# TensorE's order pinned by unit in an attention and MLP kernel, with VectorE's steps of masks and outputs queued behind each unit's maxima

## The chip, the cores and the metric

The kernel runs on one core of one Trainium2 chip. The metric is the device time of one execution in microseconds (us), as the median over several executions. Five engines work side by side, each through its own instructions in order: TensorE (PE, with its weight loads listed apart as PEld), VectorE (DVE), ScalarE (ACT), GpSimd (POOL) and SyncE (SP), which issues the DMAs. TensorE writes its results to PSUM, which is cut into banks, and the others read them from there.

## The reference

Attention in which a query sees only the keys of its own cluster, then a token-mixing and a channel-mixing MLP, then a second mixing block with a cosine and a sine of a projection. Cut to what matters:

```python
# attention: B, H, S, D = 2, 8, 768, 64; 16 clusters
q_assign = np.argmax(np.einsum('bhsd,hcd->bhsc', q_n, c_n), axis=-1)
k_assign = np.argmax(np.einsum('bhsd,hcd->bhsc', k_n, c_n), axis=-1)
mask = q_assign[:, :, :, None] == k_assign[:, :, None, :]
scores = scale * np.matmul(q, k.transpose(0, 1, 3, 2))
scores = np.where(mask, scores, -1000000000.0)
attn = np.exp(scores - np.max(scores, axis=-1, keepdims=True))
attn = attn / (np.sum(attn, axis=-1, keepdims=True) + 1e-09)
x = np.matmul(attn, v)                      # then heads side by side: (2, 768, 512)
# first block: w_tok1 768x256, w_tok2 256x768, w_ch1 512x1536, w_ch2 1536x512
h = np.maximum(x.transpose(0, 2, 1) @ w_tok1, 0.0) @ w_tok2
u = x + h.transpose(0, 2, 1)
x = u + np.maximum(u @ w_ch1, 0.0) @ w_ch2
# second block
theta = x @ w_theta
y = np.einsum('ts,bsd->btd', w_tok_r, x * np.cos(theta)) + np.einsum('ts,bsd->btd', w_tok_i, x * np.sin(theta))
u = x + y
out = u + np.maximum(u @ w_ch, 0.0)
```

## The kernel before

The attention is cut into 48 units: a head and a block of 256 of its 768 queries, three units to a head, six to a pair of heads. A unit has three kinds of work on TensorE. **Scores** (`scores`) are two halves of 128 queries, each in one of two PSUM banks `s`, each made of four products: L397 and L398, where L398 adds the cluster mask and the low parts of the split operands. VectorE takes the maximum of a half (`nm`, L400), ScalarE the exponential (`e`, L402), which reads the bank for the last time. **Transposes** (`turn`) are twelve (L417), in three groups that each fill one of three banks `t`; the first two groups are copied out by ScalarE (`p`, L420), the third by VectorE (L422). **Values** (`values`) are twelve products (L438) into the single bank `o`; ScalarE copies one half of it (`tmp`, L445) and VectorE adds the other (`xt`, L447), the last reader of that bank.

The units are staged by `SKEW = 2`: step n of the loop issues the scores of unit n, the transposes of unit n-1 and the values of unit n-2. Between them stand other things. A generator `masks` makes the masks of the next pair of heads in six pieces, two to a step (`PACE`): eight `sim` products into a bank `t` (L246), four VectorE steps, a product `pp` (L270), and `oh` and `m` (L271, L286), which DMAs from SP place in the operands of the next pair's scores. `natural` takes the finished outputs of a pair of heads back to rows: VectorE makes the reciprocal sums `ri` (L455, L456), TensorE six transposes `x` (L460) into two banks `t`, VectorE scales them into `xn` (L462). In the last steps the weights of the first MLP are loaded (`load_w`, L109 to L116, of which L109 and L110 are on ScalarE, L112 and L113 on VectorE, L116 on GpSimd) and, near the end, its first products are made by `tok_up` (`g` in PSUM, then `gh` on ScalarE, L147, and `gl` on VectorE, L148) and `tok_down` (`h`). The inputs of these are split into high and low parts `xh` (L84) and `xl` (L86). Every MLP product is three matmuls (`mm3`, L126 to L128).

A scheduler that runs when the kernel is built decides the order of the instructions on each engine. `tc.issue_after(ins)` puts whatever is issued under it behind the instruction `ins` on the same engine: an edge of order, not a semaphore. `marks` keeps such instructions by name: `marks["scores"]`, `marks["max"]`, `marks["turn"]` are the latest score product, maximum and transpose.

## Time and profile before

| | us |
|---|---|
| median of the runs shown | 665.26 (663.36, 665.26, 665.73) |
| profiled execution | 664.99 |
| its span | 663.3 |
| TensorE busy | 646.8 (98%) |
| weight loads busy | 517.7 (78%) |
| VectorE busy | 401.2 (60%) |
| ScalarE busy | 344.9 (52%) |
| GpSimd busy | 257.6 (39%) |

The span goes from the first to the last instruction of the profiled execution, and its own time is 1.7 us longer. Busy times of matmuls overlap a little, since one starts before the one ahead of it has ended, so distances are best read from start to start. In the rows below PEclk and clock stand for the granted clock of TensorE as a share of full speed, and "[0.62 <-ACT e L402]" behind a row means that the engine was idle for 0.62 us ahead of it and that ScalarE's `e` of line 402 ended this.

### The profile page before, as it was taken

To read this page: it belongs to the slowest core of one execution; us is meant where nothing else is said; L and a number is where in the kernel's file an instruction comes from. 1 tells how busy PE (TensorE), PEld (TensorE's weight loads), DVE (VectorE), ACT (ScalarE), POOL (GpSimd) and SP (SyncE) were. 2 spreads that over 40 slices of the span, in tenths; PEclk is the share of its full clock that TensorE was granted. 3 is DMA by queue.
4 is the path that set the end of the run, shared out by engine and by line. 5 is a ranking of instruction groups with operands and counts; after the bars stand their busy time and mean duration, and the time that the engine had idled before them with its cause. 6 is when DMAs were issued, how large, how long until landed. Compare 5 with 4: busy or idle time off the path is not lost.

```text
span 663.3 us, 9795 instructions
## 1 busy us (share of the span) xinstructions
PE 646.8 (98%) x3591; PEld 517.7 (78%) x3591; DVE 401.2 (60%) x649; ACT 344.9 (52%) x653; POOL 257.6 (39%) x231
## 2 busy tenths in 40 slices
PE   7999999999999989999999999999999999999998
PEld 4777777777777758878888888888887878888886
DVE  5877778687787776466665442546677694531212
ACT  5676776777767863256444320428487673320000
POOL 6230312364031131138887520603467796541000
PEclk9999999999999998999999999999999999999999
DMA  8554755444555121023433310310021424300001
GB/s 294 160 138 105 169 123 144 120 117 114 113 123 124 37 96 47 18 67 124 154 133 127 126 53 14 95 33 0 1 85 42 128 88 127 114 20 33 16 33 47
DMA packets 24207, 61.42 MB, mean 93 GB/s; under 512 B 4256, under 2 KB 7520, under 8 KB 24160
## 3 DMA queue, kind: packets, MB, share of 16 engines
q1 hardware_dynamic: 24160, 60.80, 32.3%
q8 instruction: 28, 0.46, 0.3%
q14 instruction: 19, 0.16, 0.1%
HBM read 39.65 MB, written 3.15 MB: 65 GB/s over the span
## 4 chain that ended last, share of the span: by engine, by line
PE 86%; ACT 4%; DVE 3%; POOL 3%; issue 2%; DMA 2%; SPq 0%; POOLq 0%; ACTq 0%
PE o L438 10%; PE t L417 9%; PE s L397 5%; PE r L126 5%; PE r L127 5%; PE r L128 5%; PE c L126 5%; PE c L127 5%; PE c L128 5%; PE s L398 5%; PE y L128 4%; PE y L127 4%; PE y L126 4%; PE po L126 2%; PE po L128 2%
## 5 line engine op out<-in xcount | busy, mean ns | idle before, releaser
L402 ACT ACTIVATE e<-s,nm 128x768 f32<-128x768 f32 x96 | 86.7, 905 | 29.4 <-DVE nm L400 28.1
L400 DVE TENSOR_REDUCE nm<-s 128x1 f32<-128x768 f32 x96 | 90.5, 951 | 18.9 <-PE s L398 18.0
L417 PE MATMUL t<-ident,e 128*128 128x128 f32 x576 | 80.5, 275 | 0.6 <-ACT p L420 0.5
L417 PEld LDWEIGHTS t<-ident,e 128*128 128x128 f32 x576 | 66.4, 140 | 16.0 <-issue 9.4
L397 PE MATMUL s<-k,qh 128*128 128x384 f32 x188 | 71.9, 382 | 2.5 <-ACT e L402 2.3
L438 PE MATMUL o<-p,vs 128*64 128x256 f32 x564 | 71.2, 388 | 0.0
L398 PE MATMUL s<-k,q 128*128 128x384 f32 x192 | 65.3, 343 | 2.4 <-DVE q L279 2.4
L420 ACT ACTIVATE p<-t 128x512 f32<-128x512 f32 x96 | 52.2, 594 | 25.4 <-PE t L417 25.0
L126 PE MATMUL r<-ul,c_h 128*128 128x512 f32 x144 | 56.5, 396 | 0.4 <-DVE ul L90 0.4
L126 PE MATMUL y<-zl,k_h 128*128 128x512 f32 x144 | 56.1, 390 | 0.0
L128 PE MATMUL y<-zh,k_h 128*128 128x512 f32 x144 | 56.1, 390 | 0.0
L127 PE MATMUL r<-uh,c_l 128*128 128x512 f32 x144 | 56.1, 390 | 0.0
L127 PE MATMUL y<-zh,k_l 128*128 128x512 f32 x144 | 56.0, 389 | 0.0
L127 PE MATMUL c<-c_h,rl 128*128 128x512 f32 x144 | 56.0, 390 | 0.0
L128 PE MATMUL r<-uh,c_h 128*128 128x512 f32 x144 | 56.0, 390 | 0.0
L128 PE MATMUL c<-c_h,rh 128*128 128x512 f32 x144 | 55.9, 390 | 0.0
L126 PE MATMUL c<-c_l,rh 128*128 128x512 f32 x144 | 55.2, 391 | 0.0
L438 PEld LDWEIGHTS o<-p,vs 128*64 128x64 f32 x564 | 36.3, 136 | 22.7 <-issue 5.9
L116 POOL TENSOR_TENSOR c_f<-c_f,c_raw 128x512 uint32<-128x512 uint32 x24 | 31.6, 1318 | 44.7 <-issue 31.3
L80 POOL TENSOR_SCALAR qh<-ql 128x768 fp32r<-128x768 f32 x7 | 5.8, 835 | 100.9 <-DMA qh<-qh 100.8
L397 PEld LDWEIGHTS s<-k,qh 128*128 128x128 f32 x188 | 35.4, 188 | 11.1 <-ACT e L402 5.6
L398 PEld LDWEIGHTS s<-k,q 128*128 128x128 f32 x192 | 36.7, 192 | 3.8 <-ACT k L276 3.4
(192 smaller groups left out, 1387.9 us busy)
## 6 DMA issues: line engine op xcount, KB each, us to landing
c_raw<-wc SPq DMA_DIRECT2D x24, 512.0 KB, 3.3
k_raw<-wri SPq DMA_DIRECT2D x18, 512.0 KB, 3.5
qh<-qh SPq DMA_DIRECT2D x28, 192.0 KB, 3.0
k<-kh SPq DMA_DIRECT2D x28, 192.0 KB, 3.8
ql<-qT SPq DMA_DIRECT2D x8, 384.0 KB, 3.2
kl<-kT SPq DMA_DIRECT2D x8, 384.0 KB, 4.6
vs<-v SPq DMA_DIRECT2D x16, 192.0 KB, 2.4
w_raw<-w SPq DMA_DIRECT2D x6, 512.0 KB, 4.1
```

Of the source, the lines that this page charges most:

```text
L80: nc.gpsimd.tensor_scalar(out=h, in0=x, scalar1=1.0, scalar2=0.0, op0=ALU.mult, op1=ALU.add)
L116: nc.gpsimd.tensor_tensor(out=wu, in0=wu, in1=lo, op=ALU.add)
L126: nc.tensor.matmul(ps, ah, bl, start=first and i == 0, stop=False)
L127: nc.tensor.matmul(ps, al, bh, start=False, stop=False)
L128: nc.tensor.matmul(ps, ah, bh, start=False, stop=last and i == n - 1)
L397: nc.tensor.matmul(ps[:, half, :NH], qh[:, c], k1[:, n], start=True, stop=False)
L398: marks["scores"] = nc.tensor.matmul(ps[:, half, :NH], ql[:, c], kk[:, n], start=False, stop=True)
L400: marks["max"] = nc.vector.tensor_reduce(out=nm, in_=ps[:, :, :NH], axis=AX.XY, op=ALU.max, negate=True)
L402: marks["exp"] = nc.scalar.activation(out=e.rearrange("p (a n) -> p a n", a=2), in_=ps[:, :, :NH], func=AF.Exp, bias=nm, accum_out=sums[b, ...
L417: marks["turn"] = nc.tensor.transpose(ps[:, a, i * P : i * P + P], es[i][:, kt * P : kt * P + P], ident)
L420: marks["pA"] = nc.scalar.activation(out=p, in_=ps, func=AF.Copy)
L438: nc.tensor.matmul(po[r : r + 64, :], vs[:, kt, :], pr[kt // 2][:, kt % 2, :], start=kt < 2, stop=kt >= NT - 2, tile_position=(0, r),)
```

## The change

Scores of a unit now stand behind the last values product issued (`marks["o"]`, which is new), and transposes behind the scores of their step. The steps of `natural` and, from the fourth step on, those of the mask generator are issued behind the step's last maximum, which on VectorE puts them behind it; the mask steps come after the values in the step and no longer ahead of the transposes; `natural` comes three steps after the last values of its pair and no longer one. Since the edges are on the order of instructions, no semaphore is added.

```diff
--- before.py
+++ after.py
@@ -435,7 +435,7 @@
                 po = ps[:, 256 * i : 256 * i + 256]
                 for kt in range(NT):
                     r = 64 * (kt % 2)
-                    nc.tensor.matmul(
+                    marks["o"] = nc.tensor.matmul(
                         po[r : r + 64, :], vs[:, kt, :], pr[kt // 2][:, kt % 2, :], start=kt < 2, stop=kt >= NT - 2,
                         tile_position=(0, r),
                     )
@@ -489,7 +489,8 @@
                     sums[b, h // 2] = small.tile([P, NT, 2], F32, tag="sm", bufs=2, name=f"sm{b}{h}")
                     xts[b, h // 2] = ap.tile([P, S], F32, tag="xt", bufs=2, name=f"xt{b}{h}")
                 if n != 1:
-                    es[n] = scores(b, h, u, ops[b, h])
+                    with tc.issue_after(marks["o"].ins) if "o" in marks else nullcontext():
+                        es[n] = scores(b, h, u, ops[b, h])
                 if n == 0:
                     next(first, None)
                     place(1, ms[0, 0])
@@ -514,13 +515,11 @@
                         split_pair(*pr, raws)
                     if n % 6 == PAIR_AT[2]:
                         gen = masks(*pr)
-            if n >= 3:
-                for _ in range(PACE):
-                    next(gen, None)
             if n == 42:
                 mctx.close()
             if 0 <= n - 1 < len(units):
-                prs[n - 1] = turn(*units[n - 1], es.pop(n - 1))
+                with tc.issue_after(marks["scores"].ins) if n > 2 else nullcontext():
+                    prs[n - 1] = turn(*units[n - 1], es.pop(n - 1))
             if n < 3:
                 with tc.issue_after((marks["turn"] if n else marks["scores"]).ins):
                     for _ in range(PACE):
@@ -533,10 +532,16 @@
                         values(group)
                     group = []
                 if h % 2 == 1 and u == NT // 2 - 1:
-                    late.append((n + 1, b, h // 2))
+                    late.append((n + 3, b, h // 2))
             while late and (n >= late[0][0] or n == len(units) + SKEW - 1):
                 _, b, pr = late.pop(0)
-                natural(b, pr)
+                with tc.issue_after(marks["max"].ins):
+                    natural(b, pr)
+            if n >= 3:
+
+                with tc.issue_after(marks["max"].ins):
+                    for _ in range(PACE):
+                        next(gen, None)
             if n in X_AT:
                 tok_x(0, X_AT.index(n), part, "pp")
             if n in W1_AT:
```

The first place is TensorE in a unit of the middle without extras, before. `s_1295` and `s_1304` are the two score halves of the unit, `e_1251` and `e_1260` the exponentials of the unit before it, `t_` the three transposed groups, `o_1361` the values of the unit before that.

```order
L397 MATMUL s_1295<-k_1200,qh_1199 128x384
L398 MATMUL s_1295<-k_0_151,q_0_149 128x384
L397 MATMUL s_1295<-k_1200,qh_1199 128x384
L398 MATMUL s_1295<-k_0_151,q_0_149 128x384
L417 MATMUL t_1340<-ident,e_1251 128x128 x2
L417 MATMUL t_1347<-ident,e_1251 128x128 x2
L417 MATMUL t_1354<-ident,e_1251 128x128 x2
L397 MATMUL s_1304<-k_1200,qh_1199 128x384
L398 MATMUL s_1304<-k_0_151,q_0_149 128x384
L397 MATMUL s_1304<-k_1200,qh_1199 128x384
L398 MATMUL s_1304<-k_0_151,q_0_149 128x384
L417 MATMUL t_1340<-ident,e_1260 128x128 x2
```

The same place in the changed kernel, up to the first values:

```order
L397 MATMUL s_1295<-k_1183,qh_1182 128x384
L398 MATMUL s_1295<-k_0_151,q_0_149 128x384
L397 MATMUL s_1295<-k_1183,qh_1182 128x384
L398 MATMUL s_1295<-k_0_151,q_0_149 128x384
L397 MATMUL s_1304<-k_1183,qh_1182 128x384
L398 MATMUL s_1304<-k_0_151,q_0_149 128x384
L397 MATMUL s_1304<-k_1183,qh_1182 128x384
L398 MATMUL s_1304<-k_0_151,q_0_149 128x384
L417 MATMUL t_1340<-ident,e_1251 128x128 x2
L417 MATMUL t_1340<-ident,e_1260 128x128 x2
L417 MATMUL t_1347<-ident,e_1251 128x128 x2
L417 MATMUL t_1347<-ident,e_1260 128x128 x2
```

The second half's scores have moved ahead of all transposes, and the transposes go group by group, both halves of a group one after the other. The values follow in both, unchanged.

On ScalarE the same unit stands like this before, from its first exponential to the copy of the values:

```order
L402 ACTIVATE e_1302,sm_1293<-s_1295,nm_1300 128x768
L420 ACTIVATE p_1345<-t_1340 128x512
L420 ACTIVATE p_1352<-t_1347 128x512
L402 ACTIVATE e_1311,sm_1293<-s_1304,nm_1309 128x768
L445 ACTIVATE tmp_1368<-o_1361 64x256
```

And in the changed kernel:

```order
L420 ACTIVATE p_1345<-t_1340 128x512
L402 ACTIVATE e_1302,sm_1293<-s_1295,nm_1300 128x768
L420 ACTIVATE p_1352<-t_1347 128x512
L402 ACTIVATE e_1311,sm_1293<-s_1304,nm_1309 128x768
L445 ACTIVATE tmp_1368<-o_1361 64x256
```

The first copy of the transposed scores has moved ahead of the first exponential. In four of every six units the order is now copy, exponential, copy, exponential; in the other two it stays exponential, copy, copy, exponential.

The second place is VectorE at the first weight load of the MLP, in the step of unit 42. `w_0` is the weight, `nm_2828` and `nm_2837` are the two maxima, `xt_2429` the sum of the values `o_2799` and then of the next, `o_2877`. Before:

```order
L112 TENSOR_SCALAR w_0_raw<-w_0_f 128x512
L400 TENSOR_REDUCE nm_2828<-s_2823 128x1
L113 SCALAR_TENSOR_TENSOR w_0_f<-w_0_f,w_0_raw 128x512
L447 TENSOR_TENSOR xt_2429<-o_2799,tmp_2806 64x256
L400 TENSOR_REDUCE nm_2837<-s_2832 128x1
L422 COPY p_2875<-t_2870 128x512
L447 TENSOR_TENSOR xt_2429<-o_2877,tmp_2884 64x256
```

In the changed kernel:

```order
L112 TENSOR_SCALAR w_0_raw<-w_0_f 128x512
L400 TENSOR_REDUCE nm_2828<-s_2823 128x1
L113 SCALAR_TENSOR_TENSOR w_0_f<-w_0_f,w_0_raw 128x512
L400 TENSOR_REDUCE nm_2837<-s_2832 128x1
L447 TENSOR_TENSOR xt_2429<-o_2799,tmp_2806 64x256
L422 COPY p_2875<-t_2870 128x512
L447 TENSOR_TENSOR xt_2429<-o_2877,tmp_2884 64x256
```

The addition that reads `o_2799` has moved behind the second maximum.

The third place is ScalarE at the end of the attention, where `xh` are the splits of the second batch's rows, `c_0` the first channel weight and `gh_3308` the second half of the token MLP's hidden layer. Before:

```order
L84 ACTIVATE xh_3312<-xn_72 128x512
L84 ACTIVATE xh_3316<-xn_73 128x512
L147 ACTIVATE gh_3308<-g_3267 128x512
L84 ACTIVATE xh_3320<-xn_74 128x512
L84 ACTIVATE xh_3324<-xn_75 128x512
L84 ACTIVATE xh_3328<-xn_76 128x512
L84 ACTIVATE xh_3332<-xn_77 128x512
L109 ACTIVATE c_0_f<-c_0_raw 128x512
L110 ACTIVATE c_0_raw<-c_0_raw 128x512
```

In the changed kernel:

```order
L84 ACTIVATE xh_3312<-xn_72 128x512
L84 ACTIVATE xh_3316<-xn_73 128x512
L84 ACTIVATE xh_3320<-xn_74 128x512
L84 ACTIVATE xh_3324<-xn_75 128x512
L84 ACTIVATE xh_3328<-xn_76 128x512
L84 ACTIVATE xh_3332<-xn_77 128x512
L109 ACTIVATE c_0_f<-c_0_raw 128x512
L110 ACTIVATE c_0_raw<-c_0_raw 128x512
L147 ACTIVATE gh_3308<-g_3267 128x512
```

The second `gh` has moved behind all six splits and the two steps of `c_0`; on VectorE the `gl` that belongs to it has moved in the same way behind the six `xl` and the two VectorE steps of `c_0`, and the two VectorE steps of the last `w` now begin ahead of the first `gl`.

## Rows read from the trace of the kernel before

**Rows 1.** The page: busy time of each engine, and one costly group (part 5).

```profile
PE 646.8 (98%) x3591; PEld 517.7 (78%) x3591; DVE 401.2 (60%) x649; ACT 344.9 (52%) x653; POOL 257.6 (39%) x231
...
L397 PE MATMUL s<-k,qh 128*128 128x384 f32 x188 | 71.9, 382 | 2.5 <-ACT e L402 2.3
```

**Rows 2.** Windows: stretch, length, busy (x count) PE PEld DVE ACT POOL, clock, DMA.

```profile
93.97:150.13 56.16, 55.54 (x416) 42.62 (x415) 43.55 (x77) 40.00 (x86) 22.37 (x21) 1.00 0.56 134
...
206.29:237.81 31.52, 30.69 (x224) 23.25 (x223) 24.28 (x44) 25.82 (x55) 7.69 (x7) 1.00 0.34 90
237.81:284.00 46.19, 43.62 (x220) 35.01 (x220) 28.45 (x49) 17.03 (x32) 8.95 (x9) 0.96 0.14 47
```

**Rows 3.** Timeline, all engines: start, length, engine, line, operation, count [idle before].

```profile
110.42 0.96 DVE L400 TENSOR_REDUCE nm<-s 128x1 f32<-128x768 f32 x1 [1.65 <-PE s L398]
...
111.47 0.90 ACT L402 ACTIVATE e<-s,nm 128x768 f32<-128x768 f32 x1 [0.88 <-DVE nm L400]
...
112.52 0.44 PE L397 MATMUL s<-k,qh 128*128 128x384 f32 x1 [0.62 <-ACT e L402]
...
113.32 1.47 PE L417 MATMUL t<-ident,e 128*128 128x128 f32 x12
113.96 1.09 ACT L420 ACTIVATE p<-t 128x512 f32<-128x512 f32 x2 [1.49 <-PE t L417]
114.72 1.06 PEld L438 LDWEIGHTS o<-p,vs 128*64 128x64 f32 x12 [0.17 <-issue]
114.72 1.52 PE L438 MATMUL o<-p,vs 128*64 128x256 f32 x12
114.93 0.91 ACT L402 ACTIVATE e<-s,nm 128x768 f32<-128x768 f32 x1
...
115.81 0.91 ACT L402 ACTIVATE e<-s,nm 128x768 f32<-128x768 f32 x1
```

**Rows 4.** Timeline of TensorE, one unit without extras.

```profile
119.05 1.51 PE L438 MATMUL o<-p,vs 128*64 128x256 f32 x12
120.50 0.88 PE L417 MATMUL t<-ident,e 128*128 128x128 f32 x6
121.13 0.42 PE L397 MATMUL s<-k,qh 128*128 128x384 f32 x1
121.39 0.33 PE L398 MATMUL s<-k,q 128*128 128x384 f32 x1
...
121.91 0.82 PE L417 MATMUL t<-ident,e 128*128 128x128 f32 x6
122.48 0.42 PE L397 MATMUL s<-k,qh 128*128 128x384 f32 x1
...
123.36 1.51 PE L438 MATMUL o<-p,vs 128*64 128x256 f32 x12
```

**Rows 5.** Chain of waits from 100 to 145: start, length, what.

```profile
129.19 0.78 PE sim L246 x8
...
138.61 0.81 PE x L460 x6
```

**Rows 6.** Timeline at the first weight load of the MLP.

```profile
210.33 0.42 DVE L447 TENSOR_TENSOR xt<-o,tmp 64x256 f32<-64x256 f32 x1
...
211.15 1.52 PE L438 MATMUL o<-p,vs 128*64 128x256 f32 x12
```

**Rows 7.** Timeline at the end of the attention and the first MLP.

```profile
248.39 0.42 DVE L112 TENSOR_SCALAR w_raw<-w_f 128x512 uint32<-128x512 uint32 x1
...
248.84 0.69 DVE L113 SCALAR_TENSOR_TENSOR w_f<-w_f,w_raw 128x512 uint32<-128x512 uint32 x1
...
251.81 0.69 DVE L86 TENSOR_TENSOR w_l<-w_f,w_h 128x512 fp32r<-128x512 f32 x1 [2.28 <-POOL w_h L80]
...
252.42 1.29 DVE L86 TENSOR_TENSOR xl<-xn,xh 128x512 fp32r<-128x512 f32 x2
...
256.38 0.39 PE L126 MATMUL h<-gl,w_h 128*128 128x512 f32 x1
```

## The prediction

> **What bounds the kernel now.** I read the page's busy shares first, then the window view cut where the values products of units 3, 15, 27, 39 and 46 start, then the timeline inside one block of six units, and last the chain of waits. The shares say that TensorE works 98% of the span and that no other engine passes 60%; the one idle time that the page puts down to a softmax step ahead of a score product is 2.5 us in 663 [rows 1]. An ordering change can win back idle time or shorten what two neighbours on TensorE cost each other, and nothing else, so the question is how much there is. The windows answer it for the attention loop: the three stretches of twelve units take 56.2 us each, one of them 56.16 with TensorE busy 55.54, so 0.62 us in twelve units is idle; the stretch with the weight loads (31.52 us, 30.69 busy) has 0.83, and the one behind it, with the last values and the first MLP products (46.19, 43.62), has 2.57 [rows 2].
>
> The timeline shows where the 0.62 comes from. There are two score banks, and a third score half can start only when the exponential of the first has read its bank. A half was done just ahead of 110.42, when VectorE, idle until then, began its maximum; the exponential began at 111.47, and the next half in that bank started at 112.52, with 0.62 us idle ahead of it, released by ScalarE [rows 3]. From maximum to free bank that is 2.10 us. This is the unit of the output transposes `x`, in which no transposes or values of a unit lie between the halves to cover it; elsewhere in the block they do.
>
> **The change, term by term.** The sum is made against the profiled execution itself, 664.99 us (span 663.3 and 1.7 around it); the median of the runs shown is 665.26, so the same sum on it would end 0.3 later. Nothing is removed or added: the same matmuls, copies and DMAs are issued in another order.
>
> *Order of one unit.* Start to start, a unit without extras now costs 119.05 to 123.36 = 4.31 us in the order values, transposes, scores, transposes, scores: values 1.45, transposes 0.63 + 0.57, scores 0.78 + 0.88 [rows 4]. The units that begin with scores cost 114.72 to 119.05 = 4.33 [rows 3, 4]. The new order is values, eight scores, twelve transposes. Values stay at 1.45. The first score half behind another kind of work is 0.78 to 0.80 (121.13 to 121.91; 112.52 to 113.32); its first product is longer than the others, 0.42 against 0.33, and the second half has no such first product, so 0.70. Twelve transposes in a row before values took 113.32 to 114.72 = 1.40 [rows 3, 4]. Sum 1.45 + 0.80 + 0.70 + 1.40 = 4.35. That is 0.02 to 0.04 more than now; over the 36 units from 3 to 39 about +0.7, lower bound 0.
>
> *The wait at the outputs.* In the new order twelve transposes and twelve values, 1.40 + 1.45 = 2.85 us, always lie between the second half of one unit and the first of the next, which covers the 2.10; and the VectorE steps of `natural`, two units later, stand behind the maxima. The 0.62 per twelve units goes: 3 x 0.62 = -1.9 over the 36 units, if nothing else waits instead. The six output transposes cost 0.81 now, six of the other transposes 0.63 [rows 4, 5]; between transposes they may cost the lower figure, so 0 to -0.2 in each of six blocks, 0 to -1.1 in all. What can wait instead: the transposed scores and `x` share three banks, and a bank that `xn` frees later can hold the third transpose group. No row shows such a wait; its nearest row is the 0.17 of issue ahead of the values at 114.72 [rows 3], so 0 to 0.15 per block, 0 to +0.9.
>
> *The masks.* The eight `sim` products (0.78) [rows 5] come after values, between the score halves of the next unit as the order shows. The break gives the second half its longer first product back: 0 to +0.15 per block, 0 to +0.9. Their VectorE steps come behind the maxima; `m` goes out by DMA through SP more than a unit before its first use, so the delay is covered by 4.35 us; were that cover gone, the whole delay of up to one unit would come once per pair.
>
> Units 3 to 39 together: -1.9 + 0.7 and the three that I can't price, whose ends add up to -1.1 and +1.8. From -2.3 to +0.6; I take **-1.3**, nearer to the low end because the 0.15s are made of waits that no row shows. Ahead of unit 3 the window gives no more than the same kind of idle time, **-0.25** as a guess from 3 units' share, 0 to -0.25.
>
> *The weight loads.* Here the order works against the change. At unit 42 VectorE now runs L112, maximum, L113, `xt`, maximum, `p`; after it `xt` stands behind the second maximum. `xt` is the last reader of the one values bank: it started at 210.33, and the next values at 211.15 [rows 6]. One maximum is 0.96 [rows 3]. So that values product is up to 0.96 later, and all behind it on TensorE with it. Three loads could each cost that: 0 to +2.9. The order shows it at one of them for certain; for the other two, where the pinned order leaves less between the second maximum and the copy, I take a third each: 0.96 + 0.64 = +1.6. Against it stands the stretch's own idle 0.83, of which most goes, -0.7. Together **+0.9**, from -0.8 to +2.1.
>
> *The first MLP.* The second `gl` stood behind two of the six `xl` splits and now stands behind all six and the two VectorE steps of the first channel weight. Before, the split of `w` ended at 251.81 + 0.69 = 252.50, and the products that need the second half of `g` began with the fourth triple, at 256.38, since three banks hold the first halves of three outputs [rows 7]. With six splits of 0.65 (half of 1.29), 0.42, 0.69 and, for itself, 0.69 as for the other steps of that size, it would be ready at 258.2, 1.8 late [rows 7]; if the `w` steps run earlier, since they now stand ahead of the first `gl`, it is not late at all. Between 0 and 1.8 I take **+0.7**, slightly under the middle.
>
> Sum: -1.3 - 0.25 + 0.9 + 0.7 = +0.05, so 665.0 us. The ends add up to -3.35 and +4.5: 661.6 to 669.5.
>
> **The clock.** The stretch from 237.81 has a mean granted clock of 0.96, the three shown ahead of it 1.00 [rows 2]: TensorE waits there and runs part of what follows at 1.2 instead of 2.4 GHz. Both programs wait at that place for the first `gl`, so I price no difference.
>
> **Weight loads as the measure.** The windows give weight loads 42.62 us of 56.16 beside the 55.54 of the matmuls [rows 2]. The twelve values products have weight loads of 1.06 us and still take 1.45 from the first to the next transposes [rows 3, 4]: TensorE had nothing to wait for in between. The Trainium skill, "Perfetto Trace Analysis", section "Identifying the Most-Contended Engine", says that matmul busy time is no good measure of room on TensorE, since pipelined instructions overlap, and that weight-load busy share is to be read instead. By that page a quarter of the stretch would be room, and this change might find some of it; by the start-to-start times next to nothing is. The trace of this case bears the second reading out, for these small products.
>
> **The rivals.** *Forecast: no change that can be told,* chance 0.62. What was idle is won back, and the loads and the first MLP give as much away.
>
> *Faster.* All idle time of the loop goes and the order costs nothing: -1.9 - 1.1 - 0.8 - 0.25 = -4.05, 661 us. For it: every wait in the loop has the same cause, which the change addresses [rows 3]. Against it: the order view shows `xt` moving the wrong way. Chance 0.15. *Faster by the pace of the weight loads:* if values could follow each other at 1.06 instead of 1.45 [rows 3, 4], 48 x 0.39 = -18.7, 646 us. The order of the twelve products is the same before and after, so this needs a cause that I don't see; chance 0.02. That is how the rule of the Trainium skill's page "Perfetto Trace Analysis" would come out here; the trace does not bear it out.
>
> *Slower: ScalarE becomes the bound.* In four of six units its order turns from exponential, copy, copy, exponential into copy, exponential, copy, exponential. That closes a ring: second exponential to the scores that reuse its bank 1.05 (111.47 to 112.52), scores to transposes 0.70 to 0.80, transposes to the first copy 0.64 (113.32 to 113.96), a copy 0.48 (half of 113.96 to 114.93), an exponential 0.88 (114.93 to 115.81), a copy 0.48, and again the second exponential: 4.23 to 4.33 us [rows 3]. TensorE's unit is 4.35. The slack is 0.02 to 0.12, so from some 0.1 us of added hand-over the ring sets the pace, and each further 0.1 costs 2.8 us over the 28 units with that order. At 0.15 too long it is +4.2, 669.2 us. For it: the slack is the thinnest number here, and the old order let TensorE do transposes during it. Against it: ScalarE has only 40.00 of 56.16 us busy [rows 2]. Chance 0.21.
>
> **How the numbers follow.** The predicted time is that of the forecast, 665.0. The range 661.5 to 669.5 is the two ends of the sum; it takes in both near rivals and leaves out a ring that is longer still, a longer stretch at the lower clock, and the pace of the loads, about 2 in 10. By itself the forecast has 662 to 668. A difference of 0.5%, 3.3 us, is about what a measurement of this kernel tells from none. Faster: 0.15 + 0.02 = 0.17; same 0.62; slower 0.21.
>
> **What would show it.** Twelve units of the middle at 55.6 to 56.0 us instead of 56.16, and no wait for an exponential ahead of scores, show the loop right; 57 or more, with scores waiting for `e` in most units, shows the ring. The values product behind unit 42's load starting 5.5 us or more after the one before shows the load; a wait of TensorE for the second `gl` near 256 shows the MLP term. A rise outside of these places, or a longer stretch at the lower clock, makes the prediction wrong.

## The result: slower by 1%, and the profile after

The changed kernel takes 672.14 us (671.54 to 673.21, 3 runs) against 665.26 before: a ratio of 1.0107, 95% interval 1.0085 to 1.0129. A second measurement of it, further down, gives 1.0089 (1.0067 to 1.0110). The forecast of 665.0 us with a range up to 669.5 is wrong: the change makes the kernel slower, by more than the range allowed for.

The profiled execution has a span of 669.8 us, 6.5 more than before. Part 1 of the page (busy time, share and count by engine), which answers to [rows 1]:

```profile
PE 647.8 (97%) x3591; PEld 520.3 (78%) x3591; DVE 402.8 (60%) x649; ACT 341.8 (51%) x653; POOL 258.6 (39%) x231
```

TensorE has 1.0 us more to do than before and 5.5 us more idle time. The windows, cut at the starts of the values products of units 3, 15, 27, 39 and 46 and at the first channel product, answer to [rows 2]; the columns are the same:

```profile
38.46:94.90 56.44, 56.13 (x415) 43.10 (x415) 43.45 (x77) 39.27 (x86) 12.38 (x10) 1.00 0.54 135
94.90:151.13 56.23, 55.93 (x415) 43.11 (x414) 42.96 (x77) 39.00 (x85) 15.27 (x14) 1.00 0.53 134
...
207.36:240.07 32.71, 30.09 (x223) 23.53 (x222) 23.78 (x44) 26.01 (x56) 7.67 (x7) 1.00 0.27 70
240.07:288.19 48.12, 43.64 (x218) 34.70 (x219) 29.92 (x50) 17.32 (x32) 9.32 (x9) 0.96 0.17 55
```

Twelve units in the middle take 56.23 us in place of 56.16. Their idle time has halved, from 0.62 to 0.30, as the prediction has it in kind, but TensorE's busy time has grown by 0.39. The stretch of the weight loads takes 32.71 in place of 31.52 and has 2.62 us idle in place of 0.83. Which waits end there, the view of TensorE's waits says, from unit 39 to the middle of the first MLP (line, what it waited for, total, times, longest):

```profile
PE g L126 <- DVE gl L148: 3.9, 1, 3.9
PE o L438 <- DVE xt L447: 2.1, 3, 1.2
PE h L126 <- DVE gl L148: 0.6, 1, 0.6
PE t L417 <- DVE xn L462: 0.5, 1, 0.5
```

So the wait for the first `gl` is now 3.9 us (2.6 before), values wait for `xt` three times, the second layer's product waits 0.6 for the second `gl`, and transposes 0.5 for `xn`.

Laid beside the trace before at the same instructions, the 6.5 us of span come in like this. The first values start 1.28 later. Units 0 to 3 give back 0.60. Units 3 to 39 cost 0.39, units 39 to 46 1.20. From the last values to the fourth triple of the second layer the delay grows by 2.08, from 2.24 (start 241.91 before, 244.15 after) to 4.32 (256.38, 260.70). Then nothing happens until the channel MLP, where the delay grows by 2.26 near 390 us; the rest, 0.1 less in all, is spread thin. The loop, the weight loads and the first MLP are places that the prediction named; the late first values and the channel MLP are not.

The last one is a wait of a new kind (timeline; behind a row is the idle time ahead of it and what ended it):

```profile
388.82 0.67 ACT L110 ACTIVATE th_raw<-th_raw 128x512 uint32<-128x512 uint32 x1 [4.05 <-DMA th_raw<-wth]
...
389.94 1.06 ACT L648 ACTIVATE rh<-r 128x512 fp32r<-128x512 f32 x2
...
390.65 0.47 PE L126 MATMUL c<-c_l,rh 128*128 128x512 f32 x1 [1.04 <-ACT rh L648]
...
391.94 0.50 PE L127 MATMUL c<-c_h,rl 128*128 128x512 f32 x1 [0.82 <-DVE rl L649]
```

ScalarE stands for 4.05 us behind the transfer of a weight of the next layer (`th_raw`), with the split `rh` that TensorE needs queued behind it; TensorE waits 1.04 for `rh` and 0.82 for its `rl`. Before, the view of waits has none of TensorE at that place.

### The profile page after: what moved, and what is told of

Its sections match the earlier page's. It is cut to its first block, busy times and chain, and to the rows that moved or that the text cites. A ratio compares the mean times of both kernels' runs of the same rounds, so it can differ in the third digit from the quotient of the medians.

```text
span 669.8 us, 9862 instructions
## 1 busy us (share of the span) xinstructions
PE 647.8 (97%) x3591; PEld 520.3 (78%) x3591; DVE 402.8 (60%) x649; ACT 341.8 (51%) x653; POOL 258.6 (39%) x231
## 5 line engine op out<-in xcount | busy, mean ns | idle before, releaser
L417 PE MATMUL t<-ident,e 128*128 128x128 f32 x576 | 73.5, 275 | 1.4 <-DVE xn L462 1.1
L420 ACT ACTIVATE p<-t 128x512 f32<-128x512 f32 x96 | 54.9, 596 | 38.8 <-PE t L417 38.2
L656 DVE TENSOR_TENSOR xn<-c,xn 128x512 f32<-128x512 f32 x36 | 24.4, 686 | 24.7 <-PE c L128 24.7
```

The costliest lines, as they stand in the source:

```text
L417: marks["turn"] = nc.tensor.transpose(ps[:, a, i * P : i * P + P], es[i][:, kt * P : kt * P + P], ident)
L420: marks["pA"] = nc.scalar.activation(out=p, in_=ps, func=AF.Copy)
L656: nc.vector.tensor_tensor(out=xn[t], in0=ps, in1=xn[t], op=ALU.add)
```

## The experiments

All ran against the kernel before on the same chip, five rounds each. Under the edits, a table has the numbers on which the verdicts rest. Four questions, in the order in which they were asked.

**Is it the loop or the end, the pins or the moves?** By theory A the loss is made at the end of the attention; by theory B it is made wherever TensorE is pinned. The first pair has the whole change on one side of step 41 and the old code on the other; in `e2_end_only` the conditions are turned round.

```diff
# e1_loop_only, against the changed kernel
-with tc.issue_after(marks["o"].ins) if "o" in marks else nullcontext():
+with tc.issue_after(marks["o"].ins) if "o" in marks and n < 41 else nullcontext():
-with tc.issue_after(marks["scores"].ins) if n > 2 else nullcontext():
+with tc.issue_after(marks["scores"].ins) if 2 < n < 41 else nullcontext():
-late.append((n + 3, b, h // 2))
+late.append((n + (3 if n < 41 else 1), b, h // 2))
-with tc.issue_after(marks["max"].ins):
+with tc.issue_after(marks["max"].ins) if n < 41 else nullcontext():
     natural(b, pr)
```

> The whole change up to step 40 of the loop, and the old code from step 41 on (weight loads, last outputs, first MLP). Theory A, the loss is made at the end of the attention: units 3 to 39 take as long as in the changed kernel, 0.4 us more than before, TensorE's start of the second half of the hidden layer is as early as before plus 1.1, and the total is 666.3 us (ratio 1.0015). Theory B, pinning TensorE's order costs wherever it is done: six sevenths of the loss stay, 671 us (ratio 1.009).

> The complement: the old code up to step 40, the whole change from step 41 on. Theory A: nearly the whole loss, 670.5 to 671 us (ratio 1.008), with the first gl some 2.5 us later than before and the second 3.4 later, and the products of the channel MLP waiting for their operands near 390 us if that wait follows from the lateness ahead of it. Theory B: one seventh of the loss, 666.2 us (ratio 1.0015).

`e1_loop_only` has a ratio of 0.9990 (0.9977 to 1.0002), `e2_end_only` 1.0057 (1.0040 to 1.0075): nearer to A on both, though neither of A's numbers, 1.0015 and 1.008, lies in its interval. The loop of the change costs nothing that can be told, and its end more than half of the loss.

The second pair takes the change apart by kind. `e3_pe_only` is the kernel before with the two pins alone; `e4_dve_only` is the changed kernel with both pins taken out:

```diff
# e4_dve_only, against the changed kernel
-with tc.issue_after(marks["o"].ins) if "o" in marks else nullcontext():
+with nullcontext():
-with tc.issue_after(marks["scores"].ins) if n > 2 else nullcontext():
+with nullcontext():
```

> Only the two pins on TensorE (scores behind the last values, transposes behind the scores), masks and outputs as before. Theory A: the last outputs stay where they were and the order at the first MLP is the old one, so only the weight-load steps cost: about +1.5, 667 us (ratio 1.002). Theory B: the whole loss, 672 us (ratio 1.010).

> Only the moves of masks and outputs (behind the maxima, outputs two units later), TensorE not pinned. Theory A: the late outputs fall into the last unit beside the last weight load, but the order at the first MLP is the old one: +1 to +3, 666 to 668 us (ratio 1.0015 to 1.0045). Theory B: no loss, 665.3 us (ratio 1.000).

Here A fell: the pins alone are slower (1.0068, 1.0049 to 1.0087, between A's 1.002 and B's 1.010), and the moves alone are clearly faster than the kernel before (0.9921, 0.9905 to 0.9937), which neither theory had. The change is a gain of 0.8% and a loss of some 1.8% laid over each other. In the moves' loop TensorE has no idle time at all and less to do (windows of twelve units, the columns as above):

```profile
93.43:148.35 54.92, 54.92 (x415) 42.34 (x414) 42.25 (x77) 40.30 (x85) 14.62 (x13) 1.00 0.55 138
```

That is 1.24 us less than [rows 2] have for twelve units, of which 0.62 are the idle time, and 1.31 less than in the changed kernel.

**Which of the pins?** `e6_scores_pin` has only the pin on the scores, `e7_turn_pin` only that on the transposes (each with the other one's line replaced by `nullcontext()`). `after_again` is the changed kernel once more, and `e5_outputs_early` has the outputs one step behind their values (`n + 1` for `n + 3`) with both pins.

> The changed kernel once more, for a second profile. Two of its losses may be chance: the first values started 1.28 us later than before, behind a stretch at the lower clock of 6.8 us in place of 3.4, and a channel weight's transfer took 4.6 us to land in place of 3.2, behind which TensorE waited 1.9 us near 391. Theory A (chance): both are gone in this profile and the median of many runs is 669 to 670.5 us. Theory B (they belong to the change): both are there again and the median stays at 672.

> The changed kernel with the outputs one step after the last values of their pair, as before, and not three. Theory A, the late outputs are what costs at the end: the last-but-one outputs no longer lie in the last unit, the first gl starts 5.9 us after the last values and not 7.2, and the time falls by about 2.5 against the changed kernel. Theory B, the late outputs save a wait in the loop that is worth more: transposes wait 0.7 us for xn once in six units, twelve units take 57.3 us and the time is that of the changed kernel or above.

> The changed kernel without the pin on the transposes; the scores still stand behind the last values. Theory A, the pin on the transposes costs (all eight scores stand ahead of all twelve transposes, so nothing is left between the halves to cover a wait): twelve units take 55 us, the total is 661 to 663 us (ratio 0.995). Theory B, the pin on the scores costs (a unit can't begin its scores before the values): 56.2 us for twelve units and 670 to 672 us.

> The changed kernel without the pin on the scores; the transposes still stand behind the scores of their step. Theory A: nothing is won, 56.2 us for twelve units and 669 to 672 us. Theory B: twelve units take 55 us, and the total is 661 to 663 us.

Either pin alone loses what the moves win: 1.0094 (1.0078 to 1.0110) with the scores pinned, 1.0041 (1.0026 to 1.0057) with the transposes pinned. Twelve units take 56.78 and 56.28 us. By the times, the first is as B of that run has it, and the second nearer to A of its own: each pin costs by itself. With early outputs under the pins the loop gets longer (57.13) and the end shorter (the first `gl` starts 5.40 us after the last values in place of 7.17), 1.0065 (1.0050 to 1.0081): both of its theories were right, each at its own place. `after_again` is undecided: its profile shows both unforeseen losses again, as B has it (first values at 25.32, a wait in the channel MLP), but its median, 670.40, lies where A has it, and the profiled execution is with 673.41 the slowest of the six. I come back to them below.

**Where do the pins cost, and which move wins?** By theory C the pins cost 0.65 us in six units of the loop and more at the end; by D in the loop alone. `e8_pins_loop` and `e9_pins_end` keep the moves throughout and have the pins under `n < 41` and `n >= 41`. `e10_outputs_only` and `e11_masks_only` have one of the two moves each, and no pins.

```diff
# e11_masks_only, against the kernel before
-            if n >= 3:
-                for _ in range(PACE):
-                    next(gen, None)
...
+            if n >= 3:
+                with tc.issue_after(marks["max"].ins):
+                    for _ in range(PACE):
+                        next(gen, None)
```

> The moves of masks and outputs throughout, TensorE's pins only up to step 40. Theory C, the pins cost 0.65 us per six units in the loop (the mask product and the outputs break the pinned row of scores, and the last transposes wait for a bank) and the larger part from step 41 on: twelve units take 56.2 us, the steps 39 to 46 and the first MLP are as short as without pins, 663.5 to 664.5 us (ratio 0.998). Theory D, the pins cost in the loop alone: 669 to 671 us (ratio 1.008).

> The complement: the moves throughout, the pins only from step 41 on. Theory C: twelve units take 54.9 us as without pins, 39 to 46 and the way from the last values to the first product of the second layer take 3 us more each, 666 to 668 us (ratio 1.003). Theory D: 660.5 to 662 us (ratio 0.994).

> Of the moves only that of the outputs (behind the maxima, two units later); masks as before, nothing pinned. Theory C, the outputs are what held TensorE in the loop (the idle 0.62 us per twelve units is theirs): nearly the whole gain of the moves, 661 to 662 us (ratio 0.993 to 0.995). Rival, the masks are: 664.5 to 665.5 us (ratio 0.999).

> Of the moves only that of the masks (after the values in the step, behind the maxima); outputs as before, nothing pinned. Theory C: 664 to 665.5 us (ratio 0.999). Rival: nearly the whole gain of the moves, 661 to 662 us (ratio 0.994).

`e9_pins_end` is close to what C has: 1.0012 (1.0000 to 1.0024), where C gave 1.003, and 0.9% over the moves alone. `e8_pins_loop` has the time that D gave, 1.0064 (1.0042 to 1.0087), but not for D's reason: its loop costs the 1.3 us per twelve units of C, and most of its loss is again at the end, although the pins stop at step 40 (from the values of unit 39 to the second layer's first product 51.79 us, with the moves alone 44.26). So the end can't be put down to the pins of the last steps alone.

The table below shows two forms of it. With late outputs and both pins from step 41 on (the changed kernel twice, `e2_end_only`, `e9_pins_end`), the first `gl` starts 7.14 to 7.19 us after the last values; without a pin, or with early outputs at the end, after 5.40 to 5.88 (`e12_w_late`, below, apart). In `e6_scores_pin`, `e7_turn_pin` and `e8_pins_loop` the end has another order: 16 or 17 of the 18 products of the first half of `g` stand ahead of the values of unit 46, `gl` comes 5.71 to 6.01 after the last values, and TensorE waits 3.75 to 4.53 us ahead of `x`, for the last `xt`. In `e8_pins_loop`, from VectorE's rows and then TensorE's:

```profile
247.43 1.48 DVE L112 TENSOR_SCALAR w_raw<-w_f 128x512 uint32<-128x512 uint32 x1
...
249.95 0.42 DVE L447 TENSOR_TENSOR xt<-olast,tmp 64x256 f32<-64x256 f32 x1
```

```profile
250.51 0.66 PE L460 MATMUL x<-ident,xt 128*128 128x128 f32 x2 [4.53 <-DVE xt L447]
```

From unit 39 to the second layer's first product, with some 1.6 us taken off for each 3.4 at the lower clock (an estimate, worked out in the last section), the kernels with moves and no pin take 44.0 to 44.5 us (`e13_two_banks`, below, apart), the kernel before and `e1_loop_only` 46.4 and 46.6, `e7_turn_pin` 46.4, and all others with a pin 47.5 to 48.9. Pins lengthen the end with early outputs too. Why pins that stop at step 40 change the order behind them, no run tells.

On the moves, C held for the outputs alone (0.9952, 0.9934 to 0.9970) and was wrong on the masks alone, which win as much as both (0.9918, 0.9898 to 0.9938). In the loop the two win the same.

**What passes the lateness on at the end?** `e12_w_late` is the changed kernel with the last weight of the second layer loaded behind the first `gl`; `e13_two_banks` is the moved masks alone, with two tiles for the two halves of `g`. `marks["gl00"]` is the first `gl`.

```diff
# e12_w_late, against the changed kernel
-for i in range(NT // 2):
+for i in range(NT // 2 - 1):
     w2s.append(load_w(w2[:, :, i * 256 : i * 256 + 256], f"w2_{i}", "pv"))
...
+with tc.issue_after(marks["gl00"].ins):
+    i = NT // 2 - 1
+    w2s.append(load_w(w2[:, :, i * 256 : i * 256 + 256], f"w2_{i}", "pv"))
 for s in range(NT):
     tok_x(1, s, part, "av")
# e13_two_banks, against e11_masks_only
-ps = ps_s.tile([P, 2, 512], F32, tag="s", name="g0")
 for t in range(NTT):
-    tok_up(0, t, ps[:, t, :], ...)
+    ps = ps_s.tile([P, 2, 512], F32, tag="s", name=f"g0{t}")
+    tok_up(0, t, ps[:, 0, :], ...)
```

> The changed kernel with the load of the last weight of the second layer issued behind the first gl, so that its two VectorE steps no longer stand ahead of it; by that the second gl again stands behind two of the xl splits. Theory E, these steps are what made the end of the attention longer: the first gl starts 6.0 us after the last values in place of 7.2, the second waits for nothing new, and the time falls by 2 us against the changed kernel, to 668.5 us (ratio 1.006). Rival, the late weight takes it back: its products of the second layer wait for it, and the time stays at 670 to 672 us.

> The moved masks alone (nothing pinned, outputs as before), with the two halves of the first hidden layer in two tiles of two banks instead of one tile, so that the products of the second half don't wait until the first gl has read the tile. Theory E, the wait for the first gl (2.6 us before, 3.9 in the changed kernel) is a wait for the tile and nothing else: it goes, the lower clock behind it too, and the time is 657 to 658.5 us (ratio 0.989). Rival, what is won is waited for again at the first product that needs gl: 660.4 us, as with the masks alone.

Both are nearer to E than to its rival. With the weight behind `gl` the ratio falls to 1.0026 (1.0010 to 1.0041), 4.2 and 5.4 us below the two measurements of the changed kernel, where E had 2, and the first `gl` starts 6.19 us after the last values in place of 7.17. The run moves the second `gl` as well, and its profile has no stretch at the lower clock: of the 3.38 us by which the fourth triple of the second layer is nearer to the last values, 0.98 are the first `gl`, 0.79 the second, and the rest, 1.6, goes with the clock. With two tiles the ratio is 0.9886 (0.9857 to 0.9916), the lowest median of the study at 657.55 us, though its interval overlaps that of the masks alone. In its profile TensorE's wait for `gl`, 2.6 us before, is gone from the view of waits, and the window from the last but one values on shows no idle time and no stretch at the lower clock:

```profile
232.40:273.94 41.54, 41.54 (x219) 33.58 (x219) 27.95 (x49) 16.83 (x32) 8.91 (x9) 1.00 0.16 52
```

The numbers in one place. "12 units" is from the values of unit 15 to those of unit 27, "39 to 46" likewise, "gl" is the start of the first `gl` and "layer 2" that of the second layer's first product, both counted from the last unbroken row of values products of unit 47; "39 to layer 2" is from the values of unit 39 to that first product; all are starts in each kernel's timeline. In the rows with a star the first half of `g` stands ahead of the values of unit 46, so that "39 to 46" holds some 4 us of it. "low" is how long TensorE was granted the lower clock between 200 and 300 us, which is part of "layer 2" and "39 to layer 2".

| kernel | median us | ratio | 12 units | 39 to 46 | gl | layer 2 | 39 to layer 2 | low |
|---|---|---|---|---|---|---|---|---|
| before | 665.26 | 1 | 56.15 | 31.51 | 5.88 | 12.42 | 48.05 | 3.4 |
| changed | 672.14 | 1.0107 | 56.23 | 32.71 | 7.17 | 13.72 | 50.51 | 3.4 |
| after_again | 670.40 | 1.0089 | 56.29 | 32.68 | 7.19 | 13.75 | 50.51 | 3.4 |
| e1_loop_only | 664.84 | 0.9990 | 56.26 | 31.70 | 5.86 | 12.44 | 48.23 | 3.4 |
| e2_end_only | 669.53 | 1.0057 | 56.17 | 32.23 | 7.16 | 14.53 | 50.87 | 6.8 |
| e3_pe_only | 670.42 | 1.0068 | 57.25 | 32.84 | 5.42 | 11.98 | 49.39 | 3.4 |
| e4_dve_only | 660.69 | 0.9921 | 54.93 | 29.37 | 5.86 | 10.80 | 44.26 | 0 |
| e5_outputs_early | 668.67 | 1.0065 | 57.13 | 32.54 | 5.40 | 10.35 | 47.47 | 0 |
| e6_scores_pin | 670.96 | 1.0094 | 56.78 | 36.62* | 6.01 | 13.46 | 51.38 | 6.8 |
| e7_turn_pin | 667.34 | 1.0041 | 56.28 | 35.40* | 5.71 | 12.89 | 49.64 | 6.8 |
| e8_pins_loop | 669.11 | 1.0064 | 56.27 | 37.55* | 6.01 | 12.94 | 51.79 | 6.8 |
| e9_pins_end | 665.87 | 1.0012 | 54.93 | 31.68 | 7.14 | 13.69 | 49.49 | 3.4 |
| e10_outputs_only | 662.19 | 0.9952 | 54.93 | 29.39 | 5.86 | 13.69 | 47.18 | 6.8 |
| e11_masks_only | 660.43 | 0.9918 | 54.85 | 29.61 | 5.87 | 12.43 | 46.14 | 3.4 |
| e12_w_late | 667.01 | 1.0026 | 56.26 | 32.71 | 6.19 | 11.13 | 47.95 | 0 |
| e13_two_banks | 657.55 | 0.9886 | 54.85 | 29.60 | 5.86 | 8.04 | 41.74 | 0 |

The medians are against the kernel before on each run's own chip, 664.87 to 665.90 us, so rows are best compared by their ratios.

## Why the prediction was wrong, step by step

**The loop, predicted -1.3, measured +0.39 over units 3 to 39.** The wait that it was to win is indeed won, but two of the three amounts that it could not price came out at or above their upper bounds. The first is the mask product between two score halves. In the changed kernel:

```profile
159.83 1.51 PE L438 MATMUL o<-p,vs 128*64 128x256 f32 x12
161.27 0.45 PE L397 MATMUL s<-k,qh 128*128 128x384 f32 x1
...
162.18 0.52 PE L246 MATMUL sim<-ql,cst 128*32 128x384 f32 x2
...
162.96 0.45 PE L397 MATMUL s<-k,qh 128*128 128x384 f32 x1
...
163.78 1.47 PE L417 MATMUL t<-ident,e 128*128 128x128 f32 x12
165.18 0.44 PE L438 MATMUL o<-p,vs 128*64 128x256 f32 x2
```

The unit takes 5.35 us: values 1.44, a score half 0.91, `sim` 0.78, the other half 0.82, transposes 1.40. Without `sim` it is 4.34, so `sim` costs 1.01 where its own length is 0.78: 0.23 for breaking the row, against "0 to +0.15" (the two `sim` units of twelve in the kernel before take 5.29 and 5.09, so against that kernel it is 0.16 in the mean). Unpinned, the scheduler puts the same product between values and transposes:

```profile
156.99 1.51 PE L438 MATMUL o<-p,vs 128*64 128x256 f32 x12
158.44 0.52 PE L246 MATMUL sim<-ql,cst 128*32 128x384 f32 x2
...
159.22 0.66 PE L417 MATMUL t<-ident,e 128*128 128x128 f32 x4
...
162.09 0.44 PE L438 MATMUL o<-p,vs 128*64 128x256 f32 x2
```

Here the unit takes 5.10, with the product's own 0.78 and little else above the 4.30 to 4.33 of a plain unit. The second is the bank that `xn` must free. Where the outputs are made, the changed kernel's TensorE shows:

```profile
145.82 1.52 PE L438 MATMUL o<-p,vs 128*64 128x256 f32 x12
147.27 0.66 PE L460 MATMUL x<-ident,xt 128*128 128x128 f32 x4
...
148.46 0.38 PE L460 MATMUL x<-ident,xt 128*128 128x128 f32 x2
...
149.38 1.03 PE L417 MATMUL t<-ident,e 128*128 128x128 f32 x8
150.58 0.63 PE L417 MATMUL t<-ident,e 128*128 128x128 f32 x4 [0.16 <-DVE xn L462]
151.13 0.44 PE L438 MATMUL o<-p,vs 128*64 128x256 f32 x2
```

The `x` go in two pieces, into two of the three banks `t`; eight transposes find the third bank and one that is freed in time, and the last four must wait for `xn`: 1.20 us from the eight to the four, where eight of an unbroken twelve take 0.93 (two thirds of the 1.40 above). The unit takes 5.31; with the moves alone 4.97. Together that is 0.26 + 0.34 in six units, most of the 0.65 between 28.11 and 27.46 us (from unit 24's values to unit 30's in each).

The larger error stands ahead of both. The prediction took the pins for what covers the wait at 112.52. These are TensorE's rows of that unit in the kernel before:

```profile
107.97 1.52 PE L438 MATMUL o<-p,vs 128*64 128x256 f32 x12
109.42 0.44 PE L397 MATMUL s<-k,qh 128*128 128x384 f32 x1
...
110.22 0.81 PE L460 MATMUL x<-ident,xt 128*128 128x128 f32 x6
110.88 0.33 PE L270 MATMUL pp<-eqT,ltri 128*128 128x384 bf16 x1
110.91 0.47 PE L397 MATMUL s<-k,qh 128*128 128x384 f32 x1
```

The unit takes 6.75 us, to the values at 114.72 [rows 3], and holds three score halves, at 109.42, 110.91 and, behind the wait, 112.52, with no transposes between them; further on a unit of the same twelve, 3.60 us long, has one half. That `x` and the mask product `pp` share a unit doesn't make the wait: they share one again in the next pair (at 138.54 and 139.25), with two halves, and it takes 5.11 us with no wait (137.09 to 142.20). Pins alone put two halves into every unit and lose the wait for `e`, but in `e3_pe_only` the transposes of the unit with `x` and `pp` then wait 0.74 us for `xn`, twice in twelve units. The moves do it without a pin. Move either one, and in the middle of the loop every unit has two halves, and `sim`, `x` and `pp` each a unit of its own (starts of TensorE's rows in `e11_masks_only`):

```profile
102.97 1.52 PE L438 MATMUL o<-p,vs 128*64 128x256 f32 x12
104.41 0.52 PE L246 MATMUL sim<-ql,cst 128*32 128x384 f32 x2
...
108.06 1.52 PE L438 MATMUL o<-p,vs 128*64 128x256 f32 x12
109.51 0.88 PE L460 MATMUL x<-ident,xt 128*128 128x128 f32 x6
...
113.03 1.52 PE L438 MATMUL o<-p,vs 128*64 128x256 f32 x12
114.47 0.34 PE L270 MATMUL pp<-eqT,ltri 128*128 128x384 bf16 x1
...
117.45 0.44 PE L438 MATMUL o<-p,vs 128*64 128x256 f32 x2
```

5.09 with `sim`, 4.97 with `x`, 4.42 with `pp`, and 4.30 to 4.33 without: the loop has no wait left. So the moves alone do all of it, and the pins, priced at +0.7 over 36 units, take it back: 1.31 us in twelve units. (The +0.7 was the low end of its own 0.02 to 0.04 per unit, and stands in both ends of the sum for the loop; with its own bounds, 0 and 1.4, they would have been -3.0 and +1.3.) The step that failed here is that the pins were taken for what wins the wait, and the extras in a pinned row for nearly free. The rival that the pins close a ring over ScalarE did not occur: plain units of the changed kernel take 4.34 to 4.36, as worked out (4.35).

**The weight loads, predicted +0.9, measured +1.20 over units 39 to 46.** That the size is close is luck. At the place that the prediction named, the next values come 5.58 us after those at 207.36, where before it was 4.86 (206.29 to 211.15 [rows 6]): +0.72, within the 0.96 of one maximum. The next three units are 1.20 shorter together than before, where the prediction had +0.64 for two more loads and 0.7 of idle time won back; and the last two are 1.67 longer, which it did not have. The longest step is one of these, 5.90 from the values at 231.12 (4.78 before): the late outputs of the last pair but one stand in the last unit's row.

```profile
234.78 1.27 DVE L462 TENSOR_TENSOR xn<-x,ri 128x128 f32<-128x128 f32 x6
...
235.80 1.28 PE L417 MATMUL t<-ident,e 128*128 128x128 f32 x10 [0.48 <-DVE xn L462]
235.96 0.41 DVE L447 TENSOR_TENSOR xt<-o,tmp 64x256 f32<-64x256 f32 x1
...
237.01 0.62 PEld L438 LDWEIGHTS o<-p,vs 128*64 128x64 f32 x7 [0.17 <-issue]
```

`xn` takes VectorE until 236.05 (1.27 from 234.78), the transposes wait 0.48 for it and run until the values at 237.01, and `xt` and the second maximum come behind `xn` as well. The step that failed is the one on `natural` "two units later": it was followed in the loop and not to the last pair but one, whose outputs then stand beside the last units.

**The first MLP, predicted +0.7, measured +2.1.** The prediction looked at the second `gl` and took the weight steps ahead of the first for something that could only help. They stand in its way. Before:

```profile
241.91 1.08 PE L438 MATMUL olast<-p,vs 128*64 128x256 f32 x8
```

```profile
247.79 0.68 DVE L148 SCALAR_TENSOR_TENSOR gl<-g,gh 128x512 fp32r<-128x512 f32 x1
```

In the changed kernel, where the same row of values starts at 244.15:

```profile
249.38 0.43 DVE L112 TENSOR_SCALAR w_raw<-w_f 128x512 uint32<-128x512 uint32 x1
249.72 0.28 DVE L462 TENSOR_TENSOR xn<-x,ri 128x128 f32<-128x128 f32 x1
249.92 0.68 DVE L86 TENSOR_TENSOR w_l<-w_f,w_h 128x512 fp32r<-128x512 f32 x1
250.52 0.28 DVE L462 TENSOR_TENSOR xn<-x,ri 128x128 f32<-128x128 f32 x1
250.72 0.68 DVE L113 SCALAR_TENSOR_TENSOR w_f<-w_f,w_raw 128x512 uint32<-128x512 uint32 x1
251.32 0.69 DVE L148 SCALAR_TENSOR_TENSOR gl<-g,gh 128x512 fp32r<-128x512 f32 x1
```

L112 (0.43) and L113 (0.68) of the last weight stand ahead of the first `gl`, which starts 7.17 us after the last values, 1.29 later than before. `e12_w_late` takes them out and gets 0.98 back at that place. TensorE waits for that `gl` although its next products don't read it: both halves of `g` share one tile `s` (each of the two `s` is a tile of two banks, here one to a half), and the second may be written only when the first has been read. `e13_two_banks` shows for the moved masks that this is the whole wait; two tiles in the changed kernel were not tried. The second `gl`, with 0.63 of waiting, then adds 0.8, which the prediction had as +0.7. So the step that failed here is the one that let the weight steps run ahead of the first `gl` at no cost.

**What it did not look at.** The first values start 1.28 us later than before, behind 6.8 us at the lower clock in place of 3.4. `e1_loop_only` has the same instructions as the changed kernel on each engine up to there, starts its values at 24.02 and has 3.4; `e8_pins_loop` and `e12_w_late`, the same up to there too, start them at 23.43 with 3.4 and at 25.19 with 6.8. So the profile of the change doesn't owe this to the change. `e10_outputs_only` and `e11_masks_only`, without a pin, have the 6.8. The wait in the channel MLP is there in both profiles of the changed kernel, 1.9 and 2.2 us, and, with 0.2 to 1.5 us, in all the others but the kernel before. From issue to its first use the 21st channel weight (512 KB) took 4.6 and 5.1 us in the two profiles of the changed kernel, 4.5 in `e7_turn_pin` and `e12_w_late`, and 3.1 to 4.0 in all others, and ScalarE works in order behind it. That the four share pinned transposes and late outputs throughout speaks for a part of the change in it; no run here tells how. It stays open, and so does how much of the two a usual execution of the changed kernel has, since a profile shows only one, and the second one is of the slowest of its six. Without these two, 3.0 of the 6.5 us are left, 668 us, inside the range: in this profile the range failed by what lay outside the stretches that the prediction looked at, the direction by the steps above.

**The measure of room.** The rule of the Trainium skill, "Perfetto Trace Analysis", section "Identifying the Most-Contended Engine", which goes by weight-load busy share beside the share of peak arithmetic, would by the weight loads have had a quarter of the loop as room. In the unpinned loop TensorE has no idle time, weight loads of 42.34 in 54.92 us, and the values still take 1.45 (156.99 to 158.44) up to what follows them; no order tried here found more than 1.3 of 56.2 us. But matmul busy time was no floor either: it fell from 55.54 to 54.92 with the same 415 or 416 instructions, by another order.

## What to carry to other kernels

A bound engine that is busy 99% can still gain or lose by order: count what each change of kind costs from start to start, and in the unit that waits look for what stands between two uses of the buffer that it waits for. Before pinning an order by hand, try the moves without the pins; the scheduler had places for the extras that the pins forbade. Follow each moved step to its last use, since at the end of a stage it meets work that the steady state doesn't have; and where a wait names a buffer whose values the waiting product doesn't read, look for a tile that two products share.

## What the runs showed of the hardware

A break in a row of scores costs at both of its ends: the first score behind transposes runs 0.26 us until the next one starts (121.13 to 121.39 [rows 4]), behind values 0.29 and behind `sim` 0.28 (in the changed kernel 161.27 to 161.56 and 162.96 to 163.24), and the last one ahead of `sim` 0.27 (161.91 to 162.18), the others 0.17 to 0.18. And the lower clock, 1.2 GHz, shows no fixed rule behind the long wait of the first MLP: of the 16 profiles, 12 have 3.4 or 6.8 us of it there, behind waits of TensorE of 2.5 to 4.5 us (for `gl`, in `e6_scores_pin`, `e7_turn_pin` and `e8_pins_loop` for `xt`), and three have none behind waits of 2.5 to 2.9; the one without a wait has none. While it lasts, the first layer's products start every 0.43 us in place of 0.23, so 3.4 us of it cost some 1.6.
